# Top-k attention followed by a two-layer MLP on one core: exp and norm over pairs of duos, 128-token chunks at the end, and output parts in place of warm-up matmuls

## The chip, the core and the metric

The kernel runs on one core of a Trainium2 chip. Its engines work side by side, each through its own queue in order: TensorE (PE, matmuls), VectorE (DVE), ScalarE (ACT), GpSimd (POOL) and SyncE (SP), which here only issues DMAs. Matrices for PE come from on-chip memory (SBUF); results of PE land in PSUM. The metric is the device time of the program in microseconds, as a median over runs. The kernel before took 847.75 us (median of 3 runs, 845.37 to 848.71).

## The reference

Attention over 8 batches, 8 heads, 576 tokens and head width 64. Of each row of scores only the 32 largest survive. The result, as 4608 rows of 512, goes through an MLP of width 2048 whose activation is a leaky relu with a slope per column.

```python
scores = scale * np.matmul(q, k.transpose(0, 1, 3, 2))
kth = np.partition(scores, -top_k, axis=-1)[..., -top_k:-top_k + 1]
scores = np.where(scores >= kth, scores, -1000000000.0)
attn = softmax(scores)                      # max subtracted, exp, divided by the sum
x = (attn @ v) laid out as 4608 x 512
h = x @ w_in
g = np.maximum(h, 0.0) + alpha * np.minimum(h, 0.0)
out = (g @ w_out).astype(np.float32)
```

## The kernel before, in words

**Units.** Two heads form a pair (32 pairs, four per batch). The work unit of the attention is a *duo*: 128 query rows of both heads of a pair against all 576 keys, two score matrices of 128 x 576. A batch has 16 such duos and two for the last 64 rows of its heads (marked "m"); there are 144 duos (lines 53 to 60). The main loop (line 607) has one *slot* per duo, and in slot n the duos n+2 to n-5 are in different stages. All instructions are kept in program order on each engine by the class at line 21, except where the declarations of `sm` (line 113) free the columns of one PSUM tile from each other.

**Stages of a duo.** `st_qk` (PE) forms scores in the PSUM tile ps_sc, of which there is one. `st_exit` (ACT) copies them to s_sb. `dve_slot` (DVE) takes the eight largest of each of six groups of a row (`up` and `small`), and from these a first guess p of the threshold. One slot later `st_count` (ACT) takes the sign of p - s with a running sum, which says how many elements lie above the guess, and `st_y` (POOL) multiplies s by the sign, so that DVE can take the eight elements nearest below it (p <- y) and pick the exact threshold by the count (eq, pk, KT). Another slot later `st_relu` (ACT, then POOL) pushes everything below the threshold far down. `st_exp` (line 322, slot n+3 for duo n) writes exp as bf16 into one of three w tiles, and SP issues the DMA transpose w to wT. `st_av` (line 329, slot n+5) multiplies by v, with a column of ones that gives the sum. `norm_a` and `norm_b` (lines 353 and 358), called in the middle of `dve_slot`, take the reciprocal (rz) and scale the result to x. `st_xT` (line 380) issues the DMA transpose x to xT once the four pairs of a batch are there.

**The MLP in between.** A chunk of 256 tokens (128 at the end) is queued by `mlp_ready` (line 408) in two kinds of work. A *unit* is the matmul group ph = x w_in for 512 columns' worth of output, after which DVE takes the relu into gT. A *part* is a quarter of an output block of 128 rows: one matmul for the linear share of the leaky relu (w_lin, formed at the start) and four with w_out; four parts fill pz, which ACT copies to o_sb (`o_act`) and SP stores (`o_sp`). `h_pe` issues a unit in each slot if there is one, and a second where the slot is *late* (line 617); `o_pe` issues a part at one place in each slot, and at a second where more than nine are ready or the scores are over. `keep_warm` issues four matmuls on zeros ("rest") where PE would have nothing. ph, the transposed q and k (tps) and rest share a pool of two PSUM banks; pz has one bank.

**Preparation.** q and k of a later pair are loaded (`load_one`), transposed by PE in three steps (`prep_pe`, tps) and copied to qkT by ACT (`prep_evac`); v is cast by POOL (`cast_v`). The first four pairs also copy a block of k to kd on ACT and DVE; later ones by DMA. The slots of all this are set by the table `todo`, filled by `at` from line 496 on.

**Order within a slot.** On PE: AV of n-5, a unit, a part, transposes, scores of n+2, then warm-up or part. On ACT: two signs, exit, two relus, exp of n-3, copies of qkT, scales of w_out at the start, copy of o_sb. On DVE: twelve maxima, the norm, combining steps, the maxima of y with gT between them. On POOL: two products y, two subtractions, a cast of v.

Of the kernel before, what the change touches and what calls it, by code (L numbers as in the profile page):

```python
# [35 lines left out]
def fast_path(tc, q, k, v, moe_w_in, moe_w_out, moe_alpha, out, flag):  # L36
# [5 lines left out]
    KPB = H // 2  # L42
# [11 lines left out]
    for b in range(B):  # L54
        p0 = KPB * b
        last = b == B - 1
        half = lambda j, n: [("n", p, j + i) for p in range(p0, p0 + KPB) for i in range(n)]
        tails = [("m", p0, p0 + 1), ("m", p0 + 2, p0 + 3)]
        duos += half(0, 2) + tails + half(2, 1) + half(3, 1) if last else half(0, 2) + half(2, 2) + tails
# [4 lines left out]
    with ExitStack() as ctx:  # L64
# [5 lines left out]
        s_p = pool("s", 5)  # L70
# [18 lines left out]
        def load_one(p, which, eng=SP):  # L89
            src = {"q": qv, "k": kv, "v": vv}[which]  # L90
            t = stg.tile([128, 5, 128], FP32, name=f"{which}_st", tag=f"{which}_st", bufs=2 if which == "v" else 3)
# [39 lines left out]
        v1s = [const.tile([128, 5, 2, 65], BF16, name=f"v1_{i}") for i in range(2 * KPB)]  # L131
        ws = [const.tile([128, 2, 640], BF16, name=f"w_{i}") for i in range(3)]
# [11 lines left out]
        for t in ws:  # L144
            POOL.memset(t[:, :, S:640], 0.0)
# [38 lines left out]
        def cast_v(p):  # L184
            t = st.pop(("v", p))
            d = v1s[p % (2 * KPB)]
# [33 lines left out]
        def st_exit(n):  # L220
            s = s_p.tile([128, 2, S], FP32, name="s_sb", tag="s")
# [8 lines left out]
        def dve_slot(n, f_late):  # L230
# [6 lines left out]
            eq = small[:, 128:146].rearrange("p (i c) -> p i c", i=2)  # L237
            if on(n):
# [11 lines left out]
                if on(n - 5):  # L250
                    norm_a(n - 5)
# [6 lines left out]
                if on(n - 5):  # L258
                    norm_b(n - 5)
# [3 lines left out]
            else:  # L263
                kt_sum(n - 2)
                if on(n - 5):
                    norm_a(n - 5)
                    norm_b(n - 5)
# [8 lines left out]
            if on(n - 1):  # L276
                DVE.max(out=p9[:, 0, 1:9], in_=y[:, 0, :])
# [5 lines left out]
            if on(n - 1):  # L283
                DVE.max(out=p9[:, 1, 1:9], in_=y[:, 1, :])
# [22 lines left out]
        def st_y(n):  # L307
            y = two.tile([128, 2, S], FP32, name="y", tag="y")
            sg = T.pop(("sg", n))
            for i in range(2):  # L310
                POOL.tensor_tensor(y[:, i, :], T["s", n][:, i, :], sg[:, i, :], ALU.mult)
# [10 lines left out]
        def st_exp(n):  # L322
            w = ws[n % 3]
            ACT.activation(w[:, :, 0:S], T.pop(("s", n)), AF.Exp, scale=att_scale)
            wt = three.tile([128, 10, 128], BF16, name="wT", tag="wT")
            SP.dma_start_transpose(wt, w.rearrange("p a b -> p (a b)"))
            T["wt", n] = wt

        def st_av(n):
            d = duos[n]  # L330
            wt = T.pop(("wt", n))
            xo = ps_x.tile([128, 2, 65], FP32, name="xo", tag="x")
# [14 lines left out]
            T["xo", n] = xo  # L347
# [5 lines left out]
        def norm_a(n):  # L353
            rz = two.tile([128, 2], FP32, name="rz", tag="rz")
            DVE.reciprocal(rz, T["xo", n][:, :, 64])
            T["rz", n] = rz

        def norm_b(n):
            d = duos[n]
            xo, rz = T.pop(("xo", n)), T.pop(("rz", n))  # L360
            if d[0] == "n":
                bj = (d[1] // KPB, d[2])
                if bj not in xs:
                    xs[bj] = three.tile([128, KPB * 128], BF16, name="x", tag="x")
                c0 = 128 * (d[1] % KPB)
                x = xs[bj][:, c0:c0 + 128]
            else:
                x = three.tile([128, 128], BF16, name="xm", tag="xm")
                T["xm", n] = x
            DVE.tensor_tensor(x.rearrange("p (h d) -> p h d", h=2), xo[:, :, 0:64],  # L370
                              rz.unsqueeze(2).to_broadcast([128, 2, 64]), ALU.mult)
# [8 lines left out]
        def st_xT(n):  # L380
            d = duos[n]
            b = d[1] // KPB
            if d[0] == "n":
# [3 lines left out]
                one = b == B - 1 and j >= 2  # L387
# [3 lines left out]
                SP.dma_start_transpose(t[:, :, o:o + 128], xs.pop((b, j)))  # L391
                if one or j % 2:
                    mlp_ready(t, [(S * b + 128 * (j - (0 if one else 1)), 128 if one else 256)])
            else:
                key = ("m", b // 4)
                t = chunk(key, 256)
                o = 64 * (b % 4)
# [553 lines left out]
```

## Time and profile before

| | |
|---|---|
| median of runs (3) | 847.75 us |
| profiled execution | 845.42 us |
| its span | 843.6 us |
| mean granted PE clock | 0.985 |
| PE matmul, busy | 734.5 us |
| DVE, busy | 790.7 us |
| ACT, busy | 779.7 us |
| POOL, busy | 751.1 us |
| DVE: norm, x and xm from xo (128 + 16) | 36.3 + 4.5 us, 284 ns each |
| DVE: reciprocal rz (144) | 22.0 us, 153 ns each |
| ACT: exp, w from s_sb (144) | 167.5 us, 1163 ns each |
| PE: rest (163 records) | 44.7 us |
| DMA: wT from w (144), issue to landing | 3.5 us median |

The span is the time from the first to the last record of the profiled execution; what lies around it belongs to the device time too. Busy times of one engine may overlap a little, since an instruction can begin while the one before is still draining; the distance from start to start says what an instruction costs in a row of others. A few matmul records are missing from a trace. All lines of the fast path carry the number of the recording helper, L31, so groups are told apart by tile names.

### The profile page before, as it was taken

To read this page: it belongs to the slowest core of one execution; us is meant where nothing else is said; L and a number is where in the kernel's file an instruction comes from. 1 tells how busy PE (TensorE), PEld (TensorE's weight loads), DVE (VectorE), ACT (ScalarE), POOL (GpSimd) and SP (SyncE) were. 2 spreads that over 40 slices of the span, in tenths; PEclk is the share of its full clock that TensorE was granted. 3 is DMA by queue.
4 is the path that set the end of the run, shared out by engine and by line. 5 is a ranking of instruction groups with operands and counts; after the bars stand their busy time and mean duration, and the time that the engine had idled before them with its cause. 6 is when DMAs were issued, how large, how long until landed. Compare 5 with 4: busy or idle time off the path is not lost.

```text
span 843.6 us, 18152 instructions
## 1 busy us (share of the span) xinstructions
PE 734.5 (87%) x5061; PEld 418.9 (50%) x5142; DVE 790.7 (94%) x4068; ACT 779.7 (92%) x1308; POOL 751.1 (89%) x674
## 2 busy tenths in 40 slices
PE   8678799889889898889888899888988898989896
PEld 5334355545445555445455455545555454545563
DVE  5999999999999999999999999999999999999831
ACT  5899999999999999999999999999999999999710
POOL 3899999999999999999999999999999999999800
PEclk9989999999999999999999999999999999999998
DMA  7799955556566656566565656566465655534421
GB/s 154 185 185 197 168 118 107 103 119 125 120 124 118 128 92 130 108 126 126 124 120 114 131 101 127 121 126 126 93 111 126 131 107 104 94 76 92 89 68 42
DMA packets 344461, 100.27 MB, mean 119 GB/s; under 512 B 338192, under 2 KB 338208, under 8 KB 344352
## 3 DMA queue, kind: packets, MB, share of 16 engines
q1 hardware_dynamic: 341456, 92.42, 55.8%
q0 software_dynamic: 1696, 6.30, 3.3%
q8 instruction: 43, 0.70, 0.4%
q14 instruction: 66, 0.54, 0.2%
q10 hardware_dynamic: 1200, 0.30, 0.2%
HBM read 36.71 MB, written 9.44 MB: 55 GB/s over the span
## 4 chain that ended last, share of the span: by engine, by line
DVE 63%; ACT 12%; PE 10%; POOL 6%; DMA 3%; issue 3%; SPq 1%; ACTq 0%; POOLq 0%
DVE small L31 19%; DVE p L31 17%; DVE up L31 11%; DVE gT L31 7%; ACT sg L31 4%; POOL y L31 3%; PE pz L31 3%; ACT r L31 3%; ACT s_sb L31 3%; PE ph L31 2%; DVE neg L31 2%; DVE x L31 2%; POOL s_sb L31 2%; DVE pk L31 2%; PE ps_sc L31 2%
## 5 line engine op out<-in xcount | busy, mean ns | idle before, releaser
L31 POOL TENSOR_TENSOR y<-s_sb,sg 128x576 f32<-128x576 f32 x288 | 362.5, 1280 | 46.1 <-ACT sg L31 44.0
L31 POOL TENSOR_TENSOR s_sb<-s_sb,r 128x576 f32<-128x576 f32 x288 | 362.9, 1282 | 2.6 <-ACT r L31 2.4
L31 PE MATMUL ps_sc<-qkT 64*128 64x512 f32 (+2 forms) x768 | 182.8, 573 | 71.3 <-ACT s_sb L31 69.8
L31 ACT ACTIVATE sg<-s_sb,p 128x576 bf16<-128x576 f32 x288 | 222.0, 778 | 8.8 <-DVE p L31 8.4
L31 DVE MAX8 p<-y 128x8 f32<-128x576 f32 x288 | 215.3, 748 | 4.7 <-POOL y L31 4.2
L31 DVE MAX8 small<-s_sb 128x8 f32<-128x96 f32 x864 | 216.3, 250 | 0.0
L31 DVE MAX8 up<-s_sb 128x8 f32<-128x96 f32 x864 | 211.9, 245 | 2.9 <-ACT s_sb L31 2.8
L31 ACT ACTIVATE r<-s_sb,KT 128x576 bf16<-128x576 f32 x288 | 209.2, 781 | 4.4 <-DVE KT L31 4.4
L31 ACT ACTIVATE w<-s_sb 128x1152 bf16<-128x1152 f32 x144 | 167.5, 1163 | 0.0
L31 ACT COPY s_sb<-ps_sc 128x1152 f32<-128x1152 f32 x144 | 159.8, 1109 | 2.1 <-PE ps_sc L31 2.1
L31 PE MATMUL ph<-xT,w_in_b 128*128 128x256 bf16 (+1 forms) x1216 | 152.4, 270 | 1.5 <-DVE gT L31 1.4
L31 PE MATMUL pz<-w_out_b,gT 128*128 128x512 bf16 x556 | 144.4, 381 | 3.3
L31 PE MATMUL xo<-v,wT 128*128 128x65 bf16 (+3 forms) x1600 | 126.4, 198 | 11.4 <-DMA wT<-w 9.8
L31 PEld LDWEIGHTS <-wT 128*128 128x128 bf16 (+3 forms) x1600 | 96.3, 99 | 48.9 <-DMA wT<-w 17.0
L31 PEld LDWEIGHTS ps_sc<-qkT 64*128 64x128 f32 (+1 forms) x768 | 53.6, 170 | 131.2 <-ACT s_sb L31 105.0
L31 DVE TENSOR_SCALAR gT<-ph 128x512 bf16<-128x512 f32 x144 | 97.2, 675 | 20.4 <-PE ph L31 20.3
L31 PEld LDWEIGHTS <-w_in_b 128*128 128x128 bf16 x1216 | 105.2, 98 | 21.6 <-issue 1.6
L31 PEld LDWEIGHTS ps_sc<-kd,qkT 128*128 128x128 f32 x256 | 38.5, 189 | 98.8 <-issue 96.3
L31 PEld LDWEIGHTS <-gT 128*128 128x128 bf16 x576 | 56.6, 98 | 58.3 <-issue 4.5
L31 PE MATMUL ps_sc<-kd,qkT 128*128 128x128 f32 x256 | 63.1, 329 | 0.2 <-DVE kd L31 0.2
L31 ACT ACTIVATION_READ_ACCUMULATOR sg<-s_sb,p 128x1 f32 x288 | 57.3, 199 | 0.0
L31 ACT COPY o_sb<-pz 128x512 f32<-128x512 f32 x36 | 21.0, 584 | 33.4 <-PE pz L31 25.8
(57 smaller groups left out, 679.5 us busy)
## 6 DMA issues: line engine op xcount, KB each, us to landing
k_st<-in_k_dram SPq DMA_DIRECT2D x64, 128.0 KB, 2.7
v_st<-in_v_dram SPq DMA_DIRECT2D x64, 128.0 KB, 2.8
out_dram<-o_sb SPq DMA_DIRECT2D x32, 256.0 KB, 2.6
q_st<-in_q_dram SPq DMA_DIRECT2D x62, 128.0 KB, 2.9
w_st<-in_moe_w_out_dram POOLq DMA_DIRECT2D x4, 1024.0 KB, 6.5
wT<-w SPq DMA_TRANSPOSE x144, 3.5
w_in_b<-in_moe_w_in_dram POOLq DMA_DIRECT2D x4, 512.0 KB, 5.8
k_st<-in_k_dram SPq DMA_DIRECT2D x32, 32.0 KB, 2.5
```

The source lines that it names most:

```text
L31: return self.tc.keep_in_program_order(f(*a, **kw))
```

## The change

- **Exp.** s_sb tiles now hold two duos, and so do the w tiles (two instead of three). In each even slot n one exp covers duos n-4 and n-3, followed by two DMA transposes. The s pool has 3 tiles of two duos in place of 5 of one.
- **AV and norm.** AV runs in slot n+6. xo holds two duos in one PSUM bank, and in odd slots one reciprocal and one multiplication norm both. x and xm tiles hold two row blocks; x transposes are issued in odd slots. The loop is one slot longer.
- **Chunks.** In the last batch all chunks have 128 tokens, the order of its duos puts the "m" duos behind the first block of rows, and "m" chunks collect two batches (128 tokens) where they collected four (256).
- **PE's second place.** After the scores a part is issued if more than two are ready, else a warm-up group. `o_pe` issues nothing while a finished block waits for its copy; before the scores end, that copy is issued in odd slots only.
- **Slots.** The three transposes of a pair are issued in odd slots (1, 3, 3 after its first slot, in place of 0, 1, 2) except for the last batch. A slot is late from 9 queued units on (4 from slot 118), before 12 (5 from slot 104). Scales of w_out are spread over slots 3 to 13, two in odd and one in even slots.
- **Small moves.** All kd copies and one qkT copy more are ACT's. The stages of q and k have 2 buffers in place of 3, the v tiles are 7 in place of 8, and y is split into two tiles.

```diff
-        duos += half(0, 2) + tails + half(2, 1) + half(3, 1) if last else half(0, 2) + half(2, 2) + tails
+        duos += half(0, 1) + tails + half(1, 1) + half(2, 1) + half(3, 1) if last else half(0, 2) + half(2, 2) + tails
...
-        s_p = pool("s", 5)
+        s_p = pool("s", 3)
...
-            t = stg.tile([128, 5, 128], FP32, name=f"{which}_st", tag=f"{which}_st", bufs=2 if which == "v" else 3)
+            t = stg.tile([128, 5, 128], FP32, name=f"{which}_st", tag=f"{which}_st", bufs=2)
...
-        ws = [const.tile([128, 2, 640], BF16, name=f"w_{i}") for i in range(3)]
+        ws = [const.tile([128, 2, 2, 640], BF16, name=f"w_{i}") for i in range(2)]
...
+            norm = on(n - 6) and n % 2
...
-                if on(n - 5):
-                    norm_a(n - 5)
+                if norm:
+                    norm_a(n - 6)
...
         def st_exp(n):
-            w = ws[n % 3]
-            ACT.activation(w[:, :, 0:S], T.pop(("s", n)), AF.Exp, scale=att_scale)
-            wt = three.tile([128, 10, 128], BF16, name="wT", tag="wT")
-            SP.dma_start_transpose(wt, w.rearrange("p a b -> p (a b)"))
-            T["wt", n] = wt
+            w = ws[n // 2 % 2]
+            ACT.activation(w[:, :, :, 0:S], T.pop(("s2", n // 2)), AF.Exp, scale=att_scale)
+            for i in range(2):
+                wt = three.tile([128, 10, 128], BF16, name="wT", tag="wT")
+                SP.dma_start_transpose(wt, w[:, i, :, :].rearrange("p a b -> p (a b)"))
+                T["wt", n + i] = wt
...
-            xo = ps_x.tile([128, 2, 65], FP32, name="xo", tag="x")
+            if n % 2 == 0:
+                T["xo", n // 2] = ps_x.tile([128, 2, 2, 65], FP32, name="xo", tag="x")
+            xo = T["xo", n // 2][:, n % 2, :, :]
...
-            rz = two.tile([128, 2], FP32, name="rz", tag="rz")
-            DVE.reciprocal(rz, T["xo", n][:, :, 64])
+            rz = two.tile([128, 2, 2], FP32, name="rz", tag="rz")
+            DVE.reciprocal(rz, T["xo", n // 2][:, :, :, 64])
...
-            DVE.tensor_tensor(x.rearrange("p (h d) -> p h d", h=2), xo[:, :, 0:64],
-                              rz.unsqueeze(2).to_broadcast([128, 2, 64]), ALU.mult)
+            DVE.tensor_tensor(x.rearrange("p a (h d) -> p a h d", h=2), xo[:, :, :, 0:64],
+                              rz.unsqueeze(3).to_broadcast([128, 2, 2, 64]), ALU.mult)
...
-                one = b == B - 1 and j >= 2
+                one = b == B - 1
...
-                key = ("m", b // 4)
-                t = chunk(key, 256)
+                key = ("m", b // 2)
+                t = chunk(key, 128)
...
         def o_pe():
-            if ready():
+            if ready() and not stores:
...
-                    at(s0 + u, "prep", lambda p=p, u=u: prep_pe(p, u))
+                    at(s0 + ((1, 3, 3) if b < B - 1 else (0, 1, 2))[u], "prep", lambda p=p, u=u: prep_pe(p, u))
...
-            at(3 + f // 2 if f < 8 else f - 1, "scale", lambda f=f: scale_out(f))
+            at(3 + 2 * (f // 3) + f % 3 // 2, "scale", lambda f=f: scale_out(f))
...
-        for n in range(ND + 6):
+        for n in range(ND + 7):
...
-            if on(n - 5):
-                st_av(n - 5)
+            if on(n - 6):
+                st_av(n - 6)
...
-            late = len(hq) > (12 if n < 104 else 5) or end
+            late = len(hq) > (9 if n < 118 else 4) or end
...
-            run(n, "prep", 2 if n < 4 else 1)
+            run(n, "prep", 2)
...
-            elif not did and not end:
-                keep_warm()
-            elif end or (ready() > 9 and oq[0][1] < NFT):
-                o_pe()
-            if on(n - 3):
-                st_exp(n - 3)
+            elif not (end or ready() > 2) or not o_pe():
+                if not end:
+                    keep_warm()
+            if on(n - 3) and n % 2 == 0:
+                st_exp(n - 4)
             while pend:
-                prep_evac(DVE.tensor_copy if n < 4 and len(pend) == 1 else ACT.copy)
+                prep_evac(DVE.tensor_copy if n < 4 and len(pend) == 1 and n % 2 == 0 else ACT.copy)
...
-            o_act()
-            if on(n - 5):
-                st_xT(n - 5)
+            if n % 2 or end:
+                o_act()
+            if on(n - 6) and n % 2:
+                st_xT(n - 7)
+                st_xT(n - 6)
```

## The prediction

> **What bounds the kernel now.** I read the page first: its busy shares and its chain.
>
> ```profile
> span 843.6 us, 18152 instructions
> PE 734.5 (87%) x5061; PEld 418.9 (50%) x5142; DVE 790.7 (94%) x4068; ACT 779.7 (92%) x1308; POOL 751.1 (89%) x674
> DVE 63%; ACT 12%; PE 10%; POOL 6%; DMA 3%; issue 3%; SPq 1%; ACTq 0%; POOLq 0%
> ```
>
> VectorE (DVE) carries the chain, but ScalarE (ACT) and GpSimd (POOL) are nearly as busy: average shares can't say what a saved microsecond is worth. So I cut the span into stages (columns: stage, length, then busy time of PE, PE's weight loads, DVE, ACT, POOL, and the granted clock).
>
> ```profile
> 20.00:60.00 40.00, 27.75 (x138) 12.91 (x139) 39.48 (x173) 36.76 (x64) 35.00 (x35) 0.91 0.90 186
> 60.00:160.00 100.00, 89.91 (x571) 46.55 (x580) 94.40 (x496) 99.15 (x167) 94.04 (x84) 0.97 0.75 144
> 160.00:780.00 620.00, 546.77 (x3853) 314.78 (x3914) 617.86 (x3247) 613.28 (x1026) 596.65 (x514) 1.00 0.58 115
> 791.50:836.50 45.00, 44.68 (x353) 28.18 (x356) 16.98 (x38) 10.50 (x16) 7.76 (x7) 0.97 0.29 69
> ```
>
> From 160 to 780 us DVE never rests (617.9 of 620); the stage holds 116 slots, so a slot is 5.34 us. After the last score work at 791.5 us the tail is PE's (44.7 of 45). Third, the timeline at 20 to 36 us, before any norm runs, and around 402 us, where each slot has one:
>
> ```profile
> 21.87 0.26 DVE L31 MAX8 small<-s_sb 128x8 f32<-128x96 f32 x1
> 22.85 0.75 DVE L31 MAX8 p<-y 128x8 f32<-128x576 f32 x1
> 30.37 4.75 DVE L31 COPY kd<-qkT 64x64 f32<-64x64 f32 x1
> ...
> 402.10 0.25 DVE L31 MAX8 small<-s_sb 128x8 f32<-128x96 f32 x1
> 403.27 0.75 DVE L31 MAX8 p<-y 128x8 f32<-128x576 f32 x1
> ```
>
> From the last small maximum to the first maximum of y: 0.98 us without a norm, 1.17 with one. So a norm costs DVE 0.19 us a slot, not the 0.28 + 0.15 of its two rows: the reciprocal fills a bubble that another small operation fills when it is gone. The copy of 4.75 us is alone; its two sisters took 0.19. Last, the waits from 165 to 785 us:
>
> ```profile
> PE ps_sc L31 <- ACT s_sb L31: 53.8, 69, 1.3
> POOL y L31 <- ACT sg L31: 22.0, 46, 1.1
> PE xo L31 <- DMA wT<-w: 7.7, 10, 2.1
> DVE p L31 <- POOL y L31: 1.7, 6, 0.5
> ```
>
> DVE waits for almost nothing; PE has slack, spent waiting for the score exit.
>
> **What the Trainium skill says.** "SBUF — State Buffer", section "SBUF: two separate sides": DVE and GpSimd arbitrate for one port pair, an exclusive lock held for the whole instruction, wanted by DVE operations in a two-port mode; an fp32 SBUF-to-SBUF copy is its example. The trace agrees: the 4.75 us copy stands beside an unbroken run of POOL operations and ends at 35.12, where POOL's pair of products ends (35.06). "TensorE: Matmul & The Clock Gate", section "What's actually happening": PE falls to half rate after an idle window of about 3.4 us. The trace shows the effect after less: behind an idle of 2.08 us at 249.7 us eight ph matmuls took 1.89 us instead of 1.05. "ScalarE: Activation LUTs", section "Rules for kernel authors": about 0.3 us fixed and 0.83 ns per element; here copies of 512 and 1152 elements took 584 and 1109 ns, 0.82 ns per element and 164 ns fixed.
>
> **The change, part by part.**
>
> Norm in pairs. Even slots lose 0.19 us. Odd slots hold rz of 4 and x of 256 elements. From pk (18 elements, 166 to 176 ns for its likes) to x (128, 284 ns) is about 1.05 ns per element, so 128 more cost 0.13. A pair of slots goes from 10.66 (2 x 5.33, gap-free slots at 400.26, 405.59 and 410.91) to 10.66 - 0.19 + 0.13 = 10.60; the 63 pairs outside the ACT-bound stage and the start: -4 us. Unknown is the doubled x: 0.05 to 0.2 us gives -10 to +1.
>
> Exp in pairs. One of 2304 elements replaces two of 1162 ns; start to start two cost 2.10, one 1.05 + 0.95 = 2.00. With 0.1 to 0.2 saved, ACT goes from about 10.57 to 10.45 per pair. Behind DVE this is worth nothing; in the ACT-bound stage 60 to 160 us (99.15 of 100, 9 pairs) some -1. But it is lumpy: an even slot holds signs 1.53, exit 1.0, relus 1.34, exp 2.0 = 5.9, an odd one 3.9 plus the qkT and o_sb copies. So odd slots' signs start some 0.7 us late: y's first product then ends near 3.0 to 3.2 us into the slot, and DVE wants it at 3.13. Queued behind exp are the signs, and behind those POOL's y.
>
> kd copies to ACT. The 4.75 us copy goes to ACT, which did five such in 0.24 each. DVE then meets its next hurdle at once (y1 at 35.06, wanted about 35.5): -4, at most -4.6, at least 0 if ACT or POOL has the same pause.
>
> PE. In the changed program's instruction order I count 117 warm-up groups of four idle matmuls (before: 44), at 0.87 each (45.09 to 45.96): +63 us of PE in the loop. A typical batch of 18 slots holds: 18 x (AV 0.71 + ph 0.89 + scores 1.39) = 53.8; 18 output parts x 1.08 = 19.4; 13 warm-ups 11.3; transposes 8 x 0.55 + 4 x 0.35 = 5.8; extra for tail duos 3.1: 93.4 us against DVE's 9 x 10.60 = 95.4. PE goes from 86% to 98% full. It can run about 2 us late (ph ended at 401.08 for a gT at 403.94), and bursts of two ph units plus two parts, four slots of some 25.7 against 23.5, use that up. Also two transpose groups now share an odd slot: with a pool of two ph-type banks the second waits for gT at 4.4 us into the slot, and the next ph ends about 3.4 into the following one, where gT wants it at 3.5. Together with the late signs I put +5 us of new DVE waits (0 to +25).
>
> Other moves. A parts' store waits for odd slots, and no new part starts while one waits: PE no longer stalls for o_sb (1.8 in all), nothing else follows. Staging of k and q in 2 instead of 3 buffers: the load of pair p comes two slots after the last transpose that reads its buffer, so SP's queue, loads and wT transposes behind it, doesn't stop. Two wT transposes now follow each other on SP (1.36 each, 3.5 to land); AV comes 4.8 us after exp's end, so 1 us is spare. AV lies one slot later, and the xo bank is free at the odd slot's norm, 1.5 us before the next AV. Scale copies only move in slots 3 to 14. Each of these at nothing, by that cover; without it a missed wT costs about 1 us a pair.
>
> The tail. After the last score matmul, before has 26 output parts and 21 ph units left, the changed order 17 parts and 14 units: parts no longer pile up, and the last tokens come as 128-token chunks. From DVE's last p (t0 = 791.5) before needs 52.1 us. After: PE's work up to the last AV is 4.9 (one part waits for gT) + 4.6 + 2.8 + 3.5 + 4.6 + 0.7 = 21.1, while the other chain (sign, y, KT at 5.2, relu 7.0, subtraction 8.9, exp 10.9, wT landed 14.5 and 15.9) is ready earlier. Then x 0.8, xT transpose 2.6 (its median), four rounds of ph 0.89, gT and hand-over 0.95, part less its first matmul 0.87: 10.8. Sum 35.3, plus what follows the last matmul today (836.4 to 843.6) 7.2 = 42.5: -9.6. The exact hold-ups are unknown: -3 to -15.
>
> **Sum** against the profiled execution: -4 - 1 - 4 + 5 - 9.6 = -13.6, so the span goes to 830.0 and that execution (845.42, 1.8 around its span) to 831.8. The median of the runs is 847.75, 2.3 above it; I predict 834.
>
> **Rivals.** (A) As summed: 834, own range 826 to 842. (B) PE becomes the bound: at 98% plus its ordered waits for scores, wT and gT, the pair grows. It decides from 10.60 + 18.6/63 = 10.90 us per pair (the other gains used up), and with another 0.45 us of waits a pair, under half of what PE's old waits (53.8 + 7.7 us over 58 pairs) come to, it gives 834 + 0.45 x 58 = 860. Against it: most of those waits are PE being early. (C) The tail hardly shrinks, because its chain of exp, transpose, AV and final chunk is longer than I add it (-2 to -3): 841. For it: the wait of part on gT repeats four times. (D) DVE gains all, nothing waits, and half-rate stretches go away since PE rarely idles: -4 - 1 - 4.6 - 12 - 2: 824. Against it: POOL alone needs 4 x 1.25 x 2 + 0.4 = 10.4 a pair. That exp isn't really merged is no rival: the instruction counts show 72 in place of 144.
>
> **How the numbers follow.** A 0.51, C 0.13, D 0.15, B 0.21. About 0.5% (4 us) is what this measurement can tell from none, so faster means below 843.5. A is nearly all there, C half, D all, B hardly: 0.72 faster, 0.11 same, 0.17 slower. The range 821 to 853 takes in A, C, most of D and the mild part of B, down to +0.3 us a pair.
>
> **What would show it.** Right: from 160 to 780 us DVE still above 98% with pairs near 10.6; no 4.75 us copy at 30 us; PE busy above 95% there; the tail from the last p to the end near 42 us. Wrong: DVE idle before gT (PE late) or before p (y late) of more than 10 us; pairs above 10.9; a tail above 48.

## The result, and the profile after

The changed kernel takes 879.32 us (median of 4 runs, 878.77 to 880.09) where the kernel before takes 847.01 on the same chip: a ratio of 1.038, 95% interval 1.036 to 1.041. I had predicted 834. The loss is 32.3 us; the miss is 45.

The page of the changed kernel: span, busy time by engine, and the share of each engine in the chain that ended last.

```profile
span 877.6 us, 18856 instructions
PE 794.9 (91%) x5531; PEld 448.5 (51%) x5626; DVE 784.2 (89%) x3921; ACT 776.4 (88%) x1239; POOL 752.1 (86%) x672
DVE 35%; PE 29%; POOL 13%; ACT 11%; issue 8%; DMA 3%; SPq 0%; POOLq 0%; ACTq 0%
```

DVE's total is smaller than before (784.2 against 790.7), as the change meant. But the chain no longer stays on DVE (63% before): it goes round through PE, POOL and ACT. The stages, with the columns as in the prediction (stage, length, busy PE, weight loads, DVE, ACT, POOL, granted clock):

```profile
20.00:60.00 40.00, 29.61 (x139) 13.11 (x139) 37.78 (x184) 39.94 (x67) 39.74 (x39) 0.87 0.97 189
60.00:160.00 100.00, 88.85 (x576) 47.04 (x584) 92.39 (x473) 93.68 (x152) 90.56 (x81) 0.98 0.73 143
160.00:780.00 620.00, 579.01 (x4034) 329.11 (x4104) 579.80 (x2928) 573.88 (x914) 559.42 (x482) 0.99 0.51 110
833.20:870.20 37.00, 31.28 (x303) 20.29 (x305) 12.46 (x28) 10.17 (x13) 8.99 (x8) 0.95 0.29 65
```

The third row is the finding: from 160 to 780 us DVE rests 40 us (617.86 busy before, 579.80 now), and ACT and POOL work 39 and 37 us less than before. PE is at 93%. No engine is the bound; each waits for another. The waits of that stage say for whom (columns: engine and tile that waited, for what; sum in us, times, longest; weight loads and small waits are left out):

```profile
POOL y L31 <- ACT sg L31: 56.3, 59, 2.9
PE tps L31 <- DVE gT L31: 24.4, 19, 2.3
ACT o_sb L31 <- PE pz L31: 21.0, 8, 3.4
ACT sg L31 <- DVE p L31: 18.1, 26, 1.8
DVE p L31 <- POOL y L31: 14.7, 18, 2.3
...
DVE gT L31 <- PE ph L31: 7.9, 6, 2.4
DVE small L31 <- ACT sg L31: 7.6, 16, 0.8
DVE rz L31 <- PE xo L31: 6.6, 12, 1.6
...
PE ps_sc L31 <- ACT s_sb L31: 5.1, 9, 0.9
```

The four lines of DVE make up 36.8 of its 40 us. Before, POOL's wait for the signs was 21.5 us, DVE's for y 1.7, ACT's for pz 0.4, PE's for gT 5.6, and PE waited 53.8 us for the score exit: PE was early then, and is late now.

The loss grows steadily. I followed p, the first guess that DVE writes near the end of each slot, through both timelines. After minus before it is -5.6 us at slot 6 (the kd copy is gone), -2.5 at slot 24, +3.2 at 36, +15.8 at 72, +23.5 at 108, +26.2 at 120, +41.8 at the last one, 143. From that last p to the end of the span it took 52.1 us before and takes 44.4 now.

The timeline that answers to the prediction's: kd copies at the start, then an odd slot with its norm around 440 us.

```profile
27.77 0.50 ACT L31 COPY kd<-qkT 64x64 f32<-64x64 f32 x2
...
439.19 0.25 DVE L31 MAX8 small<-s_sb 128x8 f32<-128x96 f32 x1
440.04 0.18 DVE L31 TENSOR_TENSOR small<-small,cs 128x18 f32<-128x18 f32 x1 [0.59 <-ACT sg L31]
440.13 0.17 DVE L31 RECIPROCAL rz<-xo 128x4 f32<-128x4 f32 x1
...
440.42 0.42 DVE L31 TENSOR_TENSOR x<-xo,rz 128x256 bf16<-128x256 f32 x1
...
441.20 0.75 DVE L31 MAX8 p<-y 128x8 f32<-128x576 f32 x1
```

The copy of 4.75 us is now two of 0.25 on ACT. The slot without a norm takes 5.14 us from p to p where nothing waits, as predicted (5.33 - 0.19).

The line at 440.04 is not the norm's. It is the step `eq` of `dve_slot`: it compares the counts (cs), and so needs both signs of ACT. In the source it stands behind the norm; it is one of the operations that `sm` leaves free. In this slot the compiled program has it ahead of the norm, and DVE waits 0.59 us for the signs (the bracket: idle time, and what ended it). In the kernel before it stands behind:

```profile
402.26 0.15 DVE L31 RECIPROCAL rz<-xo 128x2 f32<-128x2 f32 x1
...
403.00 0.17 DVE L31 TENSOR_TENSOR small<-small,cs 128x18 f32<-128x18 f32 x1
```

Of the 36 odd slots from 37 to 107, `eq` is ahead of the norm in 17 in the changed kernel and in none before. The diff doesn't show this; it matters below.

One place shows how a slot is lost. PE and ACT, then POOL and DVE, around 200 us (columns: start, length, engine, instruction, and in brackets the idle time before it and what ended that):

```profile
202.12 0.27 PE L31 MATMUL tps<-ident_f,k_st 64*128 64x64 f32 x1 [1.14 <-DVE gT L31]
202.38 2.17 PE L31 MATMUL ps_sc<-qkT 64*64 64x512 f32 x16
204.71 1.03 PE L31 MATMUL pz<-w_out_b,gT 128*128 128x512 bf16 x4 [0.16 <-issue]
205.77 0.59 ACT L31 COPY o_sb<-pz 128x512 f32<-128x512 f32 x1 [2.82 <-PE pz L31]
206.25 0.78 ACT L31 ACTIVATE sg<-s_sb,p 128x576 bf16<-128x576 f32 x1
...
207.20 2.52 POOL L31 TENSOR_TENSOR y<-s_sb,sg 128x576 f32<-128x576 f32 x2 [2.91 <-ACT sg L31]
208.51 0.76 DVE L31 MAX8 p<-y 128x8 f32<-128x576 f32 x1 [2.33 <-POOL y L31]
```

PE's second transpose group waits for its bank until DVE has written gT; then come the scores of a last-rows duo, and at 204.71 the last part of an output block, in the second place of the slot. ACT's copy of that block is next in ACT's queue, so ACT stands still for 2.82 us; the signs behind it are late, POOL's y is late by 2.91, DVE by 2.33. That slot lasts 7.8 us.

### The profile page after: what moved, and what is told of

It reads as the page before. It is cut to its first block, busy times and chain, and to the rows that moved or that the text cites. A ratio compares the mean times of both kernels' runs of the same rounds, so it can differ in the third digit from the quotient of the medians.

```text
span 877.6 us, 18856 instructions
## 1 busy us (share of the span) xinstructions
PE 794.9 (91%) x5531; PEld 448.5 (51%) x5626; DVE 784.2 (89%) x3921; ACT 776.4 (88%) x1239; POOL 752.1 (86%) x672
## 4 chain that ended last, share of the span: by engine, by line
DVE 35%; PE 29%; POOL 13%; ACT 11%; issue 8%; DMA 3%; SPq 0%; POOLq 0%; ACTq 0%
PE ps_sc L31 10%; DVE p L31 10%; DVE small L31 9%; POOL y L31 8%; PE pz L31 6%; DVE up L31 5%; POOL s_sb L31 5%; DVE gT L31 5%; PE ph L31 4%; PE xo L31 4%; PE rest L31 4%; ACT sg L31 4%; ACT r L31 3%; ACT s_sb L31 2%; DMA wT<-w 1%
## 5 line engine op out<-in xcount | busy, mean ns | idle before, releaser
L31 PE MATMUL ps_sc<-qkT 64*128 64x512 f32 (+2 forms) x768 | 185.2, 573 | 21.9 <-ACT s_sb L31 20.6
L31 ACT ACTIVATE w<-s_sb 128x2304 bf16<-128x2304 f32 x72 | 152.4, 2116 | 2.0 <-POOL s_sb L31 2.0
L31 PEld LDWEIGHTS <-wT 128*128 128x128 bf16 (+3 forms) x1600 | 98.7, 100 | 70.6 <-DMA wT<-w 10.8
L31 PE MATMUL rest<-idle 128*128 128x512 bf16 x434 | 121.5, 392 | 3.1 <-ACT qkT L31 1.0
L31 PEld LDWEIGHTS <-w_in_b 128*128 128x128 bf16 x1408 | 109.1, 98 | 19.7 <-DMA xT<-x 3.3
L31 PEld LDWEIGHTS ps_sc<-qkT 64*128 64x128 f32 (+1 forms) x768 | 55.4, 170 | 79.9 <-ACT s_sb L31 41.3
L31 PEld LDWEIGHTS ps_sc<-kd,qkT 128*128 128x128 f32 x256 | 39.3, 193 | 101.7 <-issue 93.4
L31 PEld LDWEIGHTS <-idle 128*128 128x128 bf16 x468 | 45.7, 101 | 36.0 <-issue 6.0
```

What stands on the lines that cost most here:

```text
L31: return self.tc.keep_in_program_order(f(*a, **kw))
```

## The experiments

All times are medians, with the ratio to the kernel before on the same chip, and its 95% interval.

### Is PE too full?

The first theory was the load of PE: the warm-up groups went from 44 to 117. First most of them are taken out of the changed kernel again (59 stay).

```diff
-                if not end:
+                if not did and not end:
                     keep_warm()
```

> The changed kernel with the rule of before for warm-ups in PE's second place: one is issued only where the slot issued no part at its first place. In the instruction order 117 groups become 59 (81 become 25 once parts exist), which takes 56 x 0.87 = 49 us of PE out of the loop. Theory 1 (PE's added load holds the loop back): nearly all of the +42 us that the loop lost comes back, about 840 us. Theory 2 (pairing the transposes in odd slots does it): at most 5 us come back, about 875. Theory 3 (exp of two duos in even slots makes ACT late): no change, about 879.

Measured: 878.54 us, 1.038 (1.034 to 1.042), no gain; at the last slot p is still 37.6 us later than in the kernel before. Alone this run settles little: PE's wait for gT ahead of tps grew from 24.4 to 42.1 us in the stage, and the granted clock there is 0.96 where the changed kernel has 0.99. The other way round, groups are added to the kernel before, 126 in all.

```diff
             elif end or (ready() > 9 and oq[0][1] < NFT):
                 o_pe()
+            elif n > 24 and n % 18 < 13:
+                keep_warm()
```

> The kernel before with a warm-up group added in PE's second place in 13 of 18 slots, from slot 25 on: 82 groups more, 71 us of PE, so that its load is that of the changed kernel (93 us per 18 slots) with everything else as before. Theory 1: it slows by a like amount as the changed loop did, to 870 to 890. If the load alone is harmless because PE has slack (10 us of 96 per batch before), 847 to 853, and theory 1 falls.

Measured: 847.36 us, 1.001 (1.000 to 1.002). Its stage from 160 to 780 us:

```profile
160.00:780.00 620.00, 608.35 (x4229) 343.22 (x4227) 616.02 (x3237) 611.60 (x1024) 594.56 (x511) 1.00 0.59 115
```

PE is busy for 608 of 620 us, more than in the changed kernel (579), and DVE still works for 616. With PE's own work at its old places, that load costs nothing. As the cause of the 32 us the theory falls; what remains is *when* PE does its work.

### Two transpose groups in one slot, exp in lumps

A *lump* below is work put together in one slot: two transpose groups, or one exp of two duos (2.1 us). First the changed kernel with one transpose group per slot, at the places of the kernel before:

```diff
-                    at(s0 + ((1, 3, 3) if b < B - 1 else (0, 1, 2))[u], "prep", lambda p=p, u=u: prep_pe(p, u))
+                    at(s0 + u, "prep", lambda p=p, u=u: prep_pe(p, u))
...
-            run(n, "prep", 2)
+            run(n, "prep", 2 if n < 4 else 1)
```

> The changed kernel with the transposes of a pair spread as before, one in each of three slots. Their number and PE's load stay. The trace of the changed kernel has PE waiting 24 + 4 us for gT and qkT before transposes between 160 and 780 us. Theory 2: most of the loss comes back, about 850. Theory 1: only those waits, partly, 865 to 875, since PE stays as full. Theory 3: no change, 879.

Measured: 868.78 us, 1.026 (1.024 to 1.029): 10.5 us of the 32 are back, and PE's wait for gT ahead of tps is gone. The edit moves something else too: `eq` is now behind the norm in 35 of the 36 odd slots, and DVE's wait for the counts falls from 7.6 to 1.3 us. How the 10.5 us divide between the two isn't shown.

The changed kernel with exp of one duo in every slot, and one wT transpose behind each:

```diff
-            ACT.activation(w[:, :, :, 0:S], T.pop(("s2", n // 2)), AF.Exp, scale=att_scale)
-            for i in range(2):
...
+            i = n % 2
+            ACT.activation(w[:, i, :, 0:S], T["s2", n // 2][:, i, :, :], AF.Exp, scale=att_scale)
...
-            if on(n - 3) and n % 2 == 0:
-                st_exp(n - 4)
+            if on(n - 3):
+                st_exp(n - 3)
```

> The changed kernel with one exp of 1152 elements in each slot in place of one of 2304 in every second; the norm stays in pairs, and so do the tiles. ACT does 72 x 0.1 to 0.2 = 7 to 14 us more work, evenly spread. Theory 3: the loop gets back 20 us or more, below 860. Theories 1 and 2: no gain, 876 to 890.

Measured: 869.59 us, 1.027 (1.025 to 1.029), 9.7 us back. Neither run lies where the theory that it was made for put it (850, and below 860): each lump has a share, none has most. In both runs ACT still waits 17 to 19 us for pz in the stage from 160 to 780 us.

### A block's last part in the second place

The kernel before never gives the second place of a slot a block's last part (`oq[0][1] < NFT`); the change dropped that. I put it back, then took out the lumps one after the other on top (the edits of the two runs above).

```diff
-            elif not (end or ready() > 2) or not o_pe():
+            elif not (end or (ready() > 2 and oq[0][1] < NFT)) or not o_pe():
```

> The changed kernel, but the second place of a slot never takes a block's last part (the condition that the kernel before has, oq[0][1] < NFT, is put back; ready() > 2 stays). Theory P (ACT stands behind a last part that PE was given in the same slot, and everything that ACT does next is late): ACT's wait for pz before the o_sb copy falls from 21 us to under 4 us in the stretch from 160 to 780 us, and the time falls from 879 to between 855 and 868 us. Rival Q (that wait only shows a PE that is late for another reason; ACT would then wait elsewhere): the wait goes but the time stays between 875 and 882 us.

Measured: 865.86 us, 1.024 (1.021 to 1.026): 13.5 us back from one condition. (In the loop it is more: at the last slot p is 18.9 us late in place of 41.8, while the stretch behind it grows from 44.4 to 51.2. The warm-up groups are 126 now, 117 before the edit.) ACT's wait for pz is no longer among the waits of the stage; POOL's for the signs and PE's for gT are smaller, and ACT's for p is larger:

```profile
POOL y L31 <- ACT sg L31: 39.7, 58, 1.3
ACT sg L31 <- DVE p L31: 24.3, 36, 2.3
PE tps L31 <- DVE gT L31: 16.3, 17, 1.6
```

> The run before it, and also one group of transposes per slot (as in the kernel before) in place of two in one odd slot. Theory P with the transposes as a separate cost (the transposes alone gave 10.5 us): 844 to 858 us. If both act through the same lateness of PE: the two gains don't add, 862 to 870 us. Rival Q: 866 to 871 us, as with the transposes alone.

Measured: 861.74 us, 1.018 (1.014 to 1.023), another 4.1, though the intervals of the two runs overlap. Under the 862 to 870 us of shared lateness by a hair, and above the 858 of added gains: so part of the 10.5 us of the transposes came through what the condition had cured already. As before, `eq` moves back behind the norm with this edit.

> The run before it, and also an exp of one duo in every slot in place of two duos in every second one (the norm stays in pairs, the 128-token chunks, the copies of kd on ACT and the extra warm-up groups stay). If the three costs add: 832 to 848 us, at or under the kernel before with 847. If the lag of AV and norm by one more slot, or the pairs of the norm, cost something by themselves: 850 to 862 us.

Measured: 847.21 us, 1.000 (0.999 to 1.001), another 14.5. All of the loss is back, with the pairs of the norm, the longer lag of AV and the warm-up groups still in. The kd copies and the new end are in too, and they gain by themselves (below), so something in this run still costs.

The reverse, in the kernel before: nothing added, but from slot 25 on a last part goes to the second place.

```diff
-            did = o_pe()
+            did = (n <= 24 or end or (ready() and oq[0][1] < NFT)) and o_pe()
...
             elif not did and not end:
-                keep_warm()
+                if n <= 24 or not o_pe():
+                    keep_warm()
```

> The kernel before, but from slot 25 on a block's last part is not issued at the first place but at the second of the same slot, behind the scores of the slot after next; ACT's copy of the block stays in that slot. Nothing is added. Theory P: ACT waits 2 to 3 us for each of some 30 blocks, and the time rises from 847 to between 860 and 885 us. Rival Q: 845 to 851 us.

Measured: 862.63 us, 1.018 (1.015 to 1.020), 16.0 us slower with the same work. Its waits from 160 to 780 us:

```profile
POOL y L31 <- ACT sg L31: 40.7, 43, 3.2
ACT o_sb L31 <- PE pz L31: 21.2, 18, 2.9
```

ACT's wait for pz is 21.2 us (0.4 before), POOL's for the signs goes from 21.5 to 40.7. So this mechanism is shown in both directions: in one it cost 13.5 us, in the other 16.0. The granted clock of the stage is 0.97 in this run and 1.00 before; how much of the 16.0 us is slower matmuls after the standstills isn't shown.

### What is left of the change

On the 847.2 us run: a finished block is copied in every slot, and last parts are allowed again near the end.

```diff
-            elif not (end or (ready() > 2 and oq[0][1] < NFT)) or not o_pe():
+            elif not (end or (ready() > 2 and (n >= 130 or oq[0][1] < NFT))) or not o_pe():
...
-            if n % 2 or end:
-                o_act()
+            o_act()
```

> The run with guard, one transpose group and one exp per slot (847.2 us), with two more edits: ACT copies a finished block in every slot, as in the kernel before, not in odd slots alone, and from slot 130 on the second place may again take a last part. In that run the stretch from the last p of DVE to the end took 48.1 us where the changed kernel takes 44.4. If the parts left over at the end made the difference: 841 to 845 us. If a last part at the second place delays the last 14 slots by as much as it saves behind them: 845.5 to 849 us.

Measured: 845.20 us, 0.997 (0.996 to 0.998), 2.0 us less, between the two readings: from the last p to the end it takes 41.6 us instead of 48.1, but p itself comes 3.3 us later.

On that, warm-up groups by the rule of the kernel before:

```diff
-                if not end:
+                if not did and not end:
                     keep_warm()
```

> The run before it, but warm-up groups at the second place only where the first place issued no part (the rule of the kernel before), so that AV doesn't stand behind such a group. DVE's 1/z waited 8.2 us for AV in the run it starts from. If the groups in front of AV are the cause: 3 to 8 us under the run before it. If PE's load costs nothing here either: within 2 us of it.

Measured: 837.23 us, 0.988 (0.985 to 0.990): faster than both kernels, and 9.8 us faster than the one before. The groups (134 before the edit, 46 with it) that cost nothing in the kernel before, and whose removal gained nothing in the changed kernel, cost 8.0 us here. DVE's wait for AV (rz for xo) falls from 7.1 to 2.5 us, POOL's for the signs from 31.7 to 26.3. Most of it lies at the end: up to slot 120 p is 1.0 us earlier, at the last slot 6.1. These are the last 23 slots, with the groups and without (columns as in the stages):

```profile
668.80:800.30 131.50, 128.95 (x990) 74.20 (x1007) 124.81 (x628) 119.84 (x197) 118.06 (x101) 1.00 0.43 94
667.80:794.20 126.40, 114.65 (x909) 67.44 (x920) 124.17 (x627) 119.35 (x197) 117.85 (x101) 0.99 0.44 97
```

PE's own work is larger there than in the kernel before (114.65 us against 107.33 in the same slots), and with the groups it is busy for 98% of the time.

Then single parts of the change in the kernel before. The kd copies of slots 0 to 3 (and one of the two DVE copies ahead of the loop likewise):

```diff
-                prep_evac(DVE.tensor_copy if n < 4 and len(pend) == 1 else ACT.copy)
+                prep_evac(DVE.tensor_copy if n < 4 and len(pend) == 1 and n % 2 == 0 else ACT.copy)
```

> The kernel before with one part of the change alone: the copies of kd in the first slots go to ACT. As predicted (DVE bounds from there to the end, a gain of 4 us stays): 842 to 844 us. If ACT and POOL run as full as DVE and DVE's gain is met by their waits: 845.5 to 848 us.

Measured: 844.11 us, 0.996 (0.995 to 0.998): 2.9 us, at the edge of the first reading.

And the end on top of that:

```diff
-        duos += half(0, 2) + tails + half(2, 1) + half(3, 1) if last else half(0, 2) + half(2, 2) + tails
+        duos += half(0, 1) + tails + half(1, 1) + half(2, 1) + half(3, 1) if last else half(0, 2) + half(2, 2) + tails
...
-                one = b == B - 1 and j >= 2
+                one = b == B - 1
...
-                key = ("m", b // 4)
-                t = chunk(key, 256)
+                key = ("m", b // 2)
+                t = chunk(key, 128)
...
```

> The run before it, and also the change's end: every block of the last batch goes in chunks of 128 tokens, the pieces of the last rows in chunks of two batches, the order of the last batch's duos as in the change. As predicted (52.1 us behind the last p become 42.5): 9 to 10 us under the run before it, 832 to 836 us. If the chunks only move work into the last slots before the last p: 841 to 846 us.

Measured: 845.82 us, 0.998 (0.996 to 0.999): no gain on top of the run before, though the stretch behind the last p falls from 53.8 to 49.8 us. p loses 5.8 us between slots 78 and 120. Of the two readings the second.

The same with the rule of the 837.2 us run for a second part in a slot:

```diff
-            elif end or (ready() > 9 and oq[0][1] < NFT):
+            elif end or (ready() > 2 and (n >= 130 or oq[0][1] < NFT)):
```

> The kernel before with the kd copies and the chunks at the end (845.8 us), and the rule of the 837.2 us run for a second part in one slot (from three ready parts on, a last part only from slot 130 on). Norm and exp stay single. Against the 837.2 us run this has no pairs in the norm. If the norm's pairs bring what was predicted (4 us): 840 to 843 us. If they bring nothing, because DVE then waits for ACT and POOL: 835.5 to 838.5 us.

Measured: 848.15 us, 1.000 (0.999 to 1.002), outside both expectations. The stretch behind the last p is the shortest of all (40.4 us), but the slots are slower. One reason is in the trace: this kernel lacks `not stores` in `o_pe`, so a new part starts while pz isn't copied, and PE waits 10.0 us for o_sb in the stage from 160 to 780 us (1.8 before). It mixes two things and tells nothing of the norm.

### Each part undone or put back in the best version

```diff
-            late = len(hq) > (9 if n < 118 else 4) or end
+            late = len(hq) > (12 if n < 104 else 5) or end
```

> The 837.2 us run with the thresholds of a late unit as in the kernel before (12, and 5 from slot 104 on, in place of 9, and 4 from slot 118 on). That run loses 4.7 us between slots 114 and 138. If the second unit of late slots causes it: 833 to 836 us. If the loss belongs to the last batch's own work: 836 to 840 us.

Measured: 838.13 us, 0.988 (0.985 to 0.992): the thresholds of a late unit make no difference.

Exp of two duos again (the edit above in reverse):

```diff
-            if on(n - 3):
-                st_exp(n - 3)
+            if on(n - 3) and n % 2 == 0:
+                st_exp(n - 4)
```

> The 837.2 us run with one edit: exp of two duos in every second slot again (2.1 us at a time). If the lump costs by itself (14.5 us where it was last taken out): 848 to 854 us. If it only cost where PE was full of warm-up groups: 835 to 841 us.

Measured: 860.76 us, 1.014 (1.010 to 1.019). One edit, 23.5 us, more than any reading expected. The timeline of ACT, POOL and DVE in this run, an even slot's exp and the odd slot behind it:

```profile
406.29 2.11 ACT L31 ACTIVATE w<-s_sb 128x2304 bf16<-128x2304 f32 x1
407.32 0.14 DVE L31 TENSOR_SCALAR p<-small 128x2 f32<-128x2 f32 x1
408.77 0.78 ACT L31 ACTIVATE sg<-s_sb,p 128x576 bf16<-128x576 f32 x1
409.72 2.52 POOL L31 TENSOR_TENSOR y<-s_sb,sg 128x576 f32<-128x576 f32 x2 [0.25 <-DVE rz L31]
411.03 0.76 DVE L31 MAX8 p<-y 128x8 f32<-128x576 f32 x1 [0.27 <-POOL y L31]
413.39 0.78 ACT L31 ACTIVATE sg<-s_sb,p 128x576 bf16<-128x576 f32 x1 [0.18 <-DVE p L31]
```

and without the lump, at the same kind of place:

```profile
408.92 1.17 ACT L31 ACTIVATE w<-s_sb 128x1152 bf16<-128x1152 f32 x1
409.84 0.14 DVE L31 TENSOR_SCALAR p<-small 128x2 f32<-128x2 f32 x1
410.60 0.80 ACT L31 ACTIVATE sg<-s_sb,p 128x576 bf16<-128x576 f32 x1
411.57 2.51 POOL L31 TENSOR_TENSOR y<-s_sb,sg 128x576 f32<-128x576 f32 x2 [0.57 <-ACT sg L31]
413.19 0.75 DVE L31 MAX8 p<-y 128x8 f32<-128x576 f32 x1
```

With the lump the signs start 1.31 us after p is written (407.46 to 408.77), because exp and a qkT copy are still ahead of them in ACT's queue; y follows, and DVE waits 0.27 us for it. Without the lump, even with two copies ahead of them, they start after 0.62, and DVE doesn't wait. As medians over the stage from 200 to 620 us, from the end of an even slot's p to the first sign and to the first maximum of y:

| | to the sign | to the maximum of y | odd slot, p to p |
|---|---|---|---|
| kernel before | 0.20 us | 3.08 us | 5.33 us |
| 837.2 us run | 0.35 us | 3.21 us | 5.46 us |
| the same with exp in lumps | 1.30 us | 3.56 us | 5.83 us |
| changed kernel | 0.85 us | 3.62 us | 5.89 us |

(The last column is over slots 36 to 107.) In the 837.2 us run DVE comes to y at 3.21 us; with the lump put back y is there 0.35 us after that, in the median of all odd slots. Even slots are at 5.14 in the last three rows. AV is late too: over the stage from 160 to 780 us DVE's wait for y grows from 0.7 to 7.7 us with the lump, and its wait for AV from 2.5 to 7.5.

The last row is a mixture. In the changed kernel the signs start 0.85 us behind p, and in the 19 odd slots with `eq` behind the norm DVE loses nothing: they last 5.46 us as a median. The 17 with `eq` ahead last 5.98; there DVE waits for the counts (5.3 us in all) and for AV (2.2). With exp of one duo in every slot the same 17 slots have `eq` ahead; they last 5.77 and wait for AV alone (4.8 us). So in the changed kernel the lump mostly reaches DVE not through y but through `eq`, which asks for the signs earlier, and in slots in which AV is late as well. The run with the condition on last parts shows the same halves (18 slots of 5.46, 18 of 5.91). Why `eq` changes its place isn't shown. With one transpose group per slot as well it is behind the norm in all of these slots, but in most a qkT copy more stands ahead of the signs; they start 1.17 us behind p, and the median odd slot takes 5.72.

The lump of exp costs 9.7, 14.5 or 23.5 us by surroundings. The 14.5 us were measured with a granted clock of 1.00 in the stage in both runs; here it is 0.97 against 0.99, so part of the 23.5 us may be slower matmuls, which isn't shown. In the even slot that follows, ACT has less to do, runs ahead of DVE and waits for p: 22.3 us, 50 times, where the 837.2 us run has 5.6, 15 times. It can't work ahead to make room for the next lump.

Two transpose groups in one slot again:

```diff
-                    at(s0 + u, "prep", lambda p=p, u=u: prep_pe(p, u))
+                    at(s0 + ((1, 3, 3) if b < B - 1 else (0, 1, 2))[u], "prep", lambda p=p, u=u: prep_pe(p, u))
...
-            run(n, "prep", 2 if n < 4 else 1)
+            run(n, "prep", 2)
```

> The 837.2 us run with one edit: two transpose groups in one odd slot again. If the lump costs by itself (4 to 10 us where it was taken out): 841 to 848 us. If it only cost together with the late copies of finished blocks: 835 to 839 us.

Measured: 846.64 us, 1.000 (0.998 to 1.002): 9.4 us for two transpose groups in a slot. PE waits again:

```profile
PE tps L31 <- DVE gT L31: 30.5, 19, 2.7
PE ps_sc L31 <- ACT s_sb L31: 21.4, 30, 2.3
```

The first of these is 2.0 us in the 837.2 us run, where PE waits for the score exit (54.4 us) as in the kernel before: there it is early. (The granted clock of the stage is 0.97 here, 0.99 there.)

The norm duo by duo, with rz of 2 and x of 128 elements in each slot, into the same tiles:

```diff
-            norm = on(n - 6) and n % 2
+            norm = on(n - 6)
...
-            rz = two.tile([128, 2, 2], FP32, name="rz", tag="rz")
-            DVE.reciprocal(rz, T["xo", n // 2][:, :, :, 64])
+            rz = two.tile([128, 2], FP32, name="rz", tag="rz")
+            DVE.reciprocal(rz, T["xo", n // 2][:, n % 2, :, 64])
...
```

> The 837.2 us run with one edit: 1/z and the product by it go duo by duo in every slot, at the same lag, with the same tiles and the same order elsewhere. If the norm's pairs bring what was predicted (0.6 of 10.66 us per pair of slots are 4 us): 840 to 843 us. If DVE then only waits less for ACT and POOL, and the pairs bring nothing: 836 to 839 us. If one product late in every second slot was a cost of the pairs: under 836 us.

Measured: 838.41 us, 0.990 (0.988 to 0.991), against 0.988 (0.985 to 0.990) with pairs. The difference of 1.2 us is inside the intervals. DVE is busy for 618.1 of the 620 us with single norms and for 611.9 with pairs: what the pairs free, DVE spends waiting.

The end as in the kernel before (its chunks, the order of the last batch's duos and the chunks of the last rows):

```diff
...
-                one = b == B - 1
+                one = b == B - 1 and j >= 2
...
```

> The 837.2 us run with one edit: the last batch's chunks, the order of its duos and the chunks of the last rows as in the kernel before (256 tokens where that kernel has them). As predicted for the end (9.6 us): 845 to 848 us. If only the 4 us come that the stretch behind the last p gained from the chunks alone: 840 to 843 us. If the shorter end is paid back in the slots ahead of it: 836 to 839 us.

Measured: 848.98 us, 1.002 (1.001 to 1.003). The end is worth 11.4 us here (848.98 and 837.23, each against its own runs of the kernel before, 847.41 and 847.01: 1.57 + 9.78). Of these 9.4 us lie behind the last p (52.7 without the new end, 43.3 with it). In the kernel before the end was worth nothing: the stretch behind the last p fell only by 4.0 us, and the slots ahead lost more than that. There the second place takes parts only from ten ready ones on; with the other rule for it the stretch fell by another 9.4 us (49.8 to 40.4).

## Why the prediction was wrong, point by point

- **Norm in pairs, -4: right in the slot, not in the time.** 5.14 for an even and 5.46 for an odd slot are what the run of 837.2 us shows as medians, 10.60 a pair as worked out. Over slots 36 to 107 its mean is 10.73 a pair, as in the kernel before, and the time shows 1.2 us, not told from none: DVE waits in the freed time.
- **Exp in pairs, -1: the worst step.** The working saw the lump, said that the odd slot's signs come 0.7 us late and that y ends at 3.0 to 3.2 us where DVE wants it at 3.13, and then put it into a shared +5. With the lump alone the signs come 1.30 us behind p (0.20 before), which puts y at 3.56 where DVE would come at 3.21 (counted from p; the working counts from the first maximum, 0.07 later). In the changed kernel itself they come at 0.85, about as foretold, and where `eq` is behind the norm y is in time; but the working has no term for `eq`, which needs the same signs and stands ahead in half of the odd slots. A margin of nothing in 72 odd slots was priced as if it would mostly hold; it cost 14.5 us in one surrounding, 9.7 and 23.5 in others.
- **kd copies, -4:** 2.9 us measured alone. Right, if a little large.
- **Two transpose groups,** part of the same +5: the mechanism was named (the second waits for gT) and is what the trace shows, 24.4 us of waits. The term was too small: 4.1, 9.4 or 10.5 us by surroundings. Of the 9.4 us `eq` is no part: it is behind the norm in 35 of 36 odd slots there.
- **"Other moves", each at nothing: the step that failed outright.** It said of the parts that a store waits for odd slots, PE no longer stalls for o_sb, and "nothing else follows". I looked at what PE no longer waits for and not at what ACT now waits for. The condition `oq[0][1] < NFT`, which the diff drops, is in no term of the working. Without it PE puts a block's last part behind the scores, and ACT's copy of the block is in the same slot's queue, ahead of the next signs: 13.5 us, and 16.0 in the reverse. This wait stood at 0.4 us before, so nothing in the profile warned of it; the diff did.
- **PE 98% full (rival B):** the load was counted about right (579.0 us in 620, at 5.64 us a slot some 95 a batch of 18; 93.4 predicted) and is not the cause, as the kernel before with 126 groups shows. (The stage's row says 88% for before, where the working says 86.) B's time, 860, was nearest, but for a reason that isn't the one found. The groups cost 8.0 us only once the lumps are gone, and most of that in the last 23 slots.
- **The tail, -9.6:** 7.7 in the changed kernel (52.1 to 44.4), 9.4 undone alone (of 11.4 in all). Right.

Of the signs of being wrong that were named, two came: DVE idle before p (14.7 us where 10 was the mark) and pairs of slots above 10.9 us (11.29 as a mean over slots 36 to 107). The third, a tail above 48 us, did not.

The steps from the changed kernel to the 837.2 us run, in the order in which they were taken: condition on last parts 13.5, transposes 4.1, exp 14.5, copies in each slot with last parts allowed near the end 2.0, warm-ups 8.0, together 42.1, from 879.3 to 837.2. In another order the single sizes are others, as shown above. Without these five the rest of the change gains 9.8 us. One by one kd gave 2.9, norm 1.2 and the end 11.4, which is 15.5; what takes the difference, the longer lag of AV for one, wasn't tried alone. So of the 17.6 us of gains foretold for these three 9.8 exist together, and moves of work within the slots, priced at +5 and at nothing, cost 42. The 821 to 853 range missed because its upper end took PE's load, not the order of the queues, as the danger.

The changed kernel loses 15.6 us in its last 23 slots alone, and the same condition has the largest share in it: ACT waits 11.6 us for pz there, and with the condition put back 7.0 us are lost. Left open: what these 7.0 are, how much the lower granted clock adds where PE stands still, and the cost of AV's longer lag. Why the warm-up groups cost 8.0 us is in part open too: that they hurt where PE has its own work to do is read from the last 23 slots, and no run took them out there alone.

## What to carry to other kernels

In this kernel three engines in a ring are all above 95% busy in the main stage (99.7, 98.9 and 96.2% before), and the total work of each decided little; what decided was whether each instruction still came before the next engine wanted it. For every instruction that a change moves later in one queue, look for the first one in another queue that waits for it (for the signs that was `eq`, not y), and then for what stands behind that one in order. Take that order from the trace and not from the source alone. A margin of a tenth of a microsecond was no cover. Merging two instructions of an engine into one saves its fixed cost (0.2 us here: 2.12 for two of 1.16) and makes what stands behind it late (about 1 us here), so it belongs where the next consumer has that much slack.

## What the runs showed that I had not expected

PE can be busy for 608 of 620 us beside DVE with 616, at no cost in time (847.36 against 847.22), where its additions are idle matmuls at the end of its slot. An operation that no line of the diff touches (`eq`) changed its place in DVE's queue in 17 of 36 odd slots; these last 5.98 us, the others 5.46. And a gain is not a property of an edit: the same end of chunks was worth 11.4 us in one kernel and nothing in another, and the same warm-up groups 0, 0 and 8 us.
